# Softcap attention with a maxout layer: a ring of three pairs of PSUM banks and fewer, longer visits per pair of heads

## The chip, the cores and the metric

The kernel runs on one core of a Trainium2 chip. The metric is the device time in microseconds. Before the change the median of three runs is 359.17 us (359.16 to 360.23). The profiled execution took 359.29 us, of which the profile covers a span of 357.5 us; all times in the profile are counted from the start of this span.

## The reference, cut to what matters

```python
batch, n_heads, seq, head_dim = (8, 12, 448, 64)
n_tokens, d_model, d_ff = (3584, 768, 1024)

def _attn_ref(q, k, v, cap):
    scale = 1.0 / np.sqrt(q.shape[-1])
    scores = scale * np.matmul(q, k.transpose(0, 1, 3, 2))
    scores = cap * np.tanh(scores / cap)
    scores = scores - np.max(scores, axis=-1, keepdims=True)
    attn = np.exp(scores)
    attn = attn / (np.sum(attn, axis=-1, keepdims=True) + 1e-09)
    return np.matmul(attn, v).astype(np.float32)

def _moe_ref(x, w1, w2, w_out):
    h1 = x @ w1
    h2 = x @ w2
    g = np.maximum(h1, h2)
    return (g @ w_out).astype(np.float32)
# x: the attention's output, heads side by side, 3584 x 768
```

There are 96 heads. Each has 448 x 448 scores, which go through tanh and exp, are summed over the keys and multiplied with the values. Then every token goes through two matrices, an elementwise maximum and a third matrix. The kernel computes the maximum as relu(x @ (w1 - w2)) + x @ w2, and multiplies w2 with w_out once, so the second layer is x @ (w1 - w2), a relu, and x @ (w2 @ w_out) + relu @ w_out.

## The kernel before

The kernel works with the scores transposed: keys lie on partitions, queries along the row. The 448 keys of a head are three blocks of 128 and one of 64; the 64 left keys of two neighbouring heads share one block. One pass of the main loop, t, handles two pairs of heads (`ab` = 0, 1), four heads in all. TensorE computes scores into PSUM, ScalarE reads them through tanh into SBUF and then takes exp, and TensorE uses the exp for the sums over the keys and for the products with the values. VectorE adds the exp of the blocks, takes reciprocals and multiplies.

[...]Scores use two tiles of two banks each, the sums and the two halves of the values two banks, the second layer the last two:

```python
    s_psum = ctx.enter_context(tc.tile_pool(name="s_psum", bufs=2, space=PSUM))
    pv_psum = ctx.enter_context(tc.tile_pool(name="pv_psum", bufs=1, space=PSUM))
    mm_psum = ctx.enter_context(tc.tile_pool(name="mm_psum", bufs=2, space=PSUM))
```

The six full key blocks and the left block of a pass are spread over four parts, two score tiles in each of three parts and one tile in part 2. There is one exp for each part:

```python
    PARTS = (((0, 0), (0, 1)), ((0, 2), (1, 0)), ((0, 3), (1, 3)), ((1, 1), (1, 2)))
    ...
    def scores(t, p, m0=0, m1=2):
        if m0 == 0:
            tanh[t, p] = att.tile([P, 4, S], bf16, name="tanh")
        if p == 2:
            s = s_psum.tile([P, 2, 512], f32, name="s")
        for m, (ab, j) in list(enumerate(PARTS[p]))[m0:m1]:
            ...
            if p == 2:
                nc.tensor.matmul(s[:, m, :S], k0[:, 3 * P : 4 * P], qTn)          # L301
                continue
            s = s_psum.tile([P, 2, 512], f32, name="s")
            for h in range(2):
                r = slice(64 * h, 64 * h + 64)
                nc.tensor.matmul(s[:, h, :S], k0[r, j * P : (j + 1) * P], qTn[r, :])   # L306
            nc.scalar.activation(tanh[t, p][:, 2 * m : 2 * m + 2, :], s[:, :, :S], AF.Tanh, scale=scale / cap)  # L307
        if p == 2:
            nc.scalar.activation(tanh[t, p][:, 0:2, :], s[:, :, :S], AF.Tanh, scale=scale / cap)   # L309

    def ex(t, p):
        n = 2 if p == 2 else 4
        expo[t, p] = att.tile([P, n, S], bf16, name=f"expo{p}", bufs=2)
        nc.scalar.activation(expo[t, p], tanh[t, p][:, 0:n, :], AF.Exp, scale=float(cap))   # L314
```

The sums (`total`) and the two halves of the values (`values`) use matmuls of 32 columns, four side by side. Then the reciprocal and the product are VectorE's:

```python
    def total(t):
        ss = pv_psum.tile([P, 512], f32, name="ss")
        ...
            for ab, h, r in HEADS:
                nc.tensor.matmul(ss[r, :S], ones[:, :32], esum[t][:, 2 * ab + h, :], start=True, stop=True)   # L356
        ...   # VectorE: transpose, reciprocal, transpose, into inv[t]

    def values(t):
        out = []
        for u, bank in enumerate(("pv", "ss")):
            ps = pv_psum.tile([P, 512], f32, name=bank)
            ...   # 12 matmuls with vp (L372), 4 with vl (L378)
            out.append(ps)
        return out

    def normalize(t, ps):
        for u in range(2):
            nc.vector.tensor_mul(x_of(t, u), ps[u][:, :S], inv[t])
```

The second layer of earlier tokens is a queue of single matmuls (`moe`, lines L406, L418 and L421). `F(n)` takes n of them from the queue and puts them into TensorE's program at that place; what is left at the end follows in one piece. The order is the program's own: nothing is rescheduled. The main loop, cut to the order of these calls for t over 2:

```python
    for t in range(1, NQ):
        if more: scores(t + 1, 0)
        ex(t, 3);               F(6)
        ...                     # loads, transposing DMA
        F(8); add(t, 1, 0); F(2)
        if more: scores(t + 1, 1); ex(t + 1, 0)
        F(4); add(t, 1, 1); F(4); add(t, 0, 2); F(4); add(t, 1, 2); F(4)
        if more: scores(t + 1, 2); ex(t + 1, 1); F(5); add(t + 1, 0, 0)
        F(5)
        total(t)
        if more: scores(t + 1, 3); ex(t + 1, 2); add(t + 1, 0, 1)
        normalize(t, values(t))
        ...                     # casts on GpSimd
        F(3)
    F(10 ** 9)
```

Of the kernel before, what the change touches and what calls it, by code (L numbers as in the profile page):

```python
# [10 lines left out]
def kernel(  # L11
# [11 lines left out]
    nc = tc.nc  # L23
# [26 lines left out]
    xpool = ctx.enter_context(tc.tile_pool(name="xpool", bufs=2))  # L50
    opool = ctx.enter_context(tc.tile_pool(name="opool", bufs=OB))
    s_psum = ctx.enter_context(tc.tile_pool(name="s_psum", bufs=2, space=PSUM))
    pv_psum = ctx.enter_context(tc.tile_pool(name="pv_psum", bufs=1, space=PSUM))
    mm_psum = ctx.enter_context(tc.tile_pool(name="mm_psum", bufs=2, space=PSUM))


# [8 lines left out]
    vl = [const.tile([P, L, P], bf16, name=f"vl{i}") for i in range(2)]  # L65
    ones = const.tile([P, 64], bf16, name="ones")
    ones2 = const.tile([P, 2, 64], bf16, name="ones2")
    mark = const.tile([1, 1], bf16, name="mark")


    kqf = [const.tile([P, L, 8, P], bf16, name=f"kqf{i}") for i in range(2)]
# [210 lines left out]

    PARTS = (((0, 0), (0, 1)), ((0, 2), (1, 0)), ((0, 3), (1, 3)), ((1, 1), (1, 2)))
    LP = {c: (p, 2 * m if p != 2 else m) for p, cs in enumerate(PARTS) for m, c in enumerate(cs)}

    def scores(t, p, m0=0, m1=2):

        if m0 == 0:  # L290
            tanh[t, p] = att.tile([P, 4, S], bf16, name="tanh")
        if p == 2:
            s = s_psum.tile([P, 2, 512], f32, name="s")
        for m, (ab, j) in list(enumerate(PARTS[p]))[m0:m1]:
            i = 2 * t + ab
            g = i // L
            k0 = qkT[g][:, i % L, :, :].rearrange("p j c -> p (j c)")
            o = Q0 + (64 * (i // NP % 2) if g >= NT else 0)
            qTn = k0[:, o : o + S]
            if p == 2:  # L300
                nc.tensor.matmul(s[:, m, :S], k0[:, 3 * P : 4 * P], qTn)  # L301
                continue
            s = s_psum.tile([P, 2, 512], f32, name="s")
            for h in range(2):
                r = slice(64 * h, 64 * h + 64)
                nc.tensor.matmul(s[:, h, :S], k0[r, j * P : (j + 1) * P], qTn[r, :])  # L306
            nc.scalar.activation(tanh[t, p][:, 2 * m : 2 * m + 2, :], s[:, :, :S], AF.Tanh, scale=scale / cap)  # L307
        if p == 2:
            nc.scalar.activation(tanh[t, p][:, 0:2, :], s[:, :, :S], AF.Tanh, scale=scale / cap)  # L309

    def ex(t, p):
        n = 2 if p == 2 else 4
        expo[t, p] = att.tile([P, n, S], bf16, name=f"expo{p}", bufs=2)
        nc.scalar.activation(expo[t, p], tanh[t, p][:, 0:n, :], AF.Exp, scale=float(cap))  # L314

    def e_of(t, ab, j):
        p, m = LP[ab, j]
        return expo[t, p][:, m : m + (1 if j == NJ else 2), :]

    esum = {}  # L320

    def add(t, ab, step):

        if t < NS or t >= NQ:
            return
        if t not in esum:
            esum[t] = att.tile([P, 4, S], bf16, name="esum")
        d = esum[t][:, 2 * ab : 2 * ab + 2, :]
        if step == 2:

            r = slice(64 * ab, 64 * ab + 64)
            d = esum[t][r, ab::2, :]
            nc.vector.tensor_add(d, d, expo[t, 2][r, :, :])  # L333
        elif step == 0:
            nc.vector.tensor_add(d, e_of(t, ab, 1 if ab else 0), e_of(t, ab, 2 if ab else 1))  # L335
        else:
            nc.vector.tensor_add(d, d, e_of(t, ab, 0 if ab else 2))  # L337

    HEADS = [(m // 2, m % 2, slice(32 * m, 32 * m + 32)) for m in range(4)]
    NB = S // 32  # L340
# [1 line left out]

    def total(t):

        ss = pv_psum.tile([P, 512], f32, name="ss")
        if t < NS:
            for j in range(NJ):
                for ab, h, r in HEADS:
                    nc.tensor.matmul(
                        ss[r, :S], ones[:, :32], e_of(t, ab, j)[:, h, :], start=(j == 0), stop=False  # L350
                    )
            for ab, h, r in HEADS:
                nc.tensor.matmul(ss[r, :S], ones2[:, h, :32], expo[t, 2][:, ab, :], start=False, stop=True)
        else:
            for ab, h, r in HEADS:
                nc.tensor.matmul(ss[r, :S], ones[:, :32], esum[t][:, 2 * ab + h, :], start=True, stop=True)  # L356
        st = att.tile([P, NB, 32], f32, name="st", bufs=1)
        nc.vector.transpose(st.rearrange("p b c -> p (b c)"), ss[:, :S])  # L358
        rs = att.tile([P, NB, 1], f32, name="rs", bufs=2)
        nc.vector.reciprocal(rs, st[:, :, 0:1])  # L360
        inv[t] = att.tile([P, S], f32, name="inv", bufs=2)
        nc.vector.transpose(inv[t].rearrange("p (b c) -> p b c", c=32), rs.to_broadcast([P, NB, 32]))

    def values(t):

        out = []
        for u, bank in enumerate(("pv", "ss")):
            ps = pv_psum.tile([P, 512], f32, name=bank)
            for j in range(NJ):
                for ab, h, r in HEADS:  # L370
                    g, n = divmod(2 * t + ab, L)
                    nc.tensor.matmul(  # L372
                        ps[r, :S], vp[g % 2][:, 2 * n + h, j, u::2], e_of(t, ab, j)[:, h, :],
                        start=(j == 0), stop=False,
                    )
            for ab, h, r in HEADS:
                g, n = divmod(2 * t + ab, L)
                nc.tensor.matmul(  # L378
                    ps[r, :S], vl[g % 2][:, n, 64 * h + u : 64 * h + 64 : 2], expo[t, 2][:, ab, :], start=False, stop=True
                )  # L380
            out.append(ps)
        return out

    xT = {}
# [6 lines left out]

    def normalize(t, ps):
        for u in range(2):
            nc.vector.tensor_mul(x_of(t, u), ps[u][:, :S], inv[t])  # L394

    gT = {}

# [98 lines left out]
    cast(nc.vector, 0, "k", 1, L)  # L496
    cast(nc.vector, 0, "q", 1, L)
    scores(0, 0)
    scores(0, 1, 0, 1)
    ex(0, 0)  # L500
    transposes(1)
    scores(0, 1, 1, 2)
    ex(0, 1)
    transposes(2)
    scores(0, 2)
    ex(0, 2)
    for _ in turn_w2(0):
        pass
    scores(0, 3)
    ex(0, 3)  # L510
    cast(nc.gpsimd, 1, "k")
    cast(nc.gpsimd, 1, "q")
    for c in range(2, KC):
# [9 lines left out]

    def premultiply_first(f0, f1):
        if f0 == 0:
            first[0] = pv_psum.tile([P, 512], f32, name="pv")
            first[1] = pv_psum.tile([P, 512], f32, name="ss")
        for f in range(f0, f1):
            for half in range(2):
                nc.tensor.matmul(  # L530
                    first[half][:, : DM // 2],
                    w2T[0][:, f * P : (f + 1) * P],
                    wo_sb[:, f, half * (DM // 2) : (half + 1) * (DM // 2)],
                    start=(f == 0), stop=(f == FC - 1),
                )
        if f1 == FC:
            for half in range(2):
                nc.vector.tensor_copy(
                    wm_sb[:, 0, half * (DM // 2) : (half + 1) * (DM // 2)], first[half][:, : DM // 2]
                )  # L540
# [10 lines left out]
    cast(nc.gpsimd, 1, "v")  # L551
    cast(nc.gpsimd, 2, "k")
    cast(nc.gpsimd, 2, "q")
    premultiply_first(0, 2)
    scores(1, 1)
    ex(1, 0)
    premultiply_first(2, 4)
    transposes(4)
    scores(1, 2)
    ex(1, 1)  # L560
    premultiply_first(4, 6)
    transposes(5)
    scores(1, 3)
    ex(1, 2)
    cross(2)
    load(3, "k")
    load(3, "q")
# [2 lines left out]
    for c in range(1, KC):  # L570
        if c + 1 < KC:
            fill_q.append(turn_w2(c + 1))
        fill_q.append(premultiply(c))
    scores(2, 0)
    ex(1, 3)
    total(0)
    F(3)
    normalize(0, values(0))
    F(2)

    for t in range(1, NQ):
        i = 2 * t
        more = t + 1 < NQ
        F(24 if t == 2 else 0)
        if t > 1 and more:
            scores(t + 1, 0)
        if t > 1:
            ex(t, 3)
            F(6)
        if t in crosses:  # L590
            cross(crosses[t])
# [7 lines left out]
            cast(nc.gpsimd, 3, "v")  # L599
        if t > 2:  # L600
            extra(i)
        F(8 if t > 1 else 0)
        add(t, 1, 0)
        F(2 if t > 1 else 0)
        if more:
            scores(t + 1, 1)
            ex(t + 1, 0)
        F(4)
        add(t, 1, 1)
        F(4)  # L610
        if t == 2:
            cast(nc.gpsimd, 2, "v")
            load(3, "v")
        add(t, 0, 2)
        F(4)
        add(t, 1, 2)
        F(4)
        if more:
            scores(t + 1, 2)
            ex(t + 1, 1)  # L620
            F(5)
            add(t + 1, 0, 0)
        if t == 1:
            for c in range(4):
                subtract(c, nc.gpsimd)
# [2 lines left out]
            extra(5)  # L628
        if t > 2:
            extra(i + 1)  # L630
        F(5)
        total(t)
        if more:
            scores(t + 1, 3)
            ex(t + 1, 2)
            add(t + 1, 0, 1)
        else:
            F(12)
        normalize(t, values(t))
        if casts[t]:  # L640
            nc.gpsimd.tensor_copy(mark, x_of(t, 1)[:1, :1])  # L641
            for g, what in casts[t]:
                cast(nc.gpsimd, g, what)
        if t % 3 == 2:
            fill_q.append(moe(t // 3))
        F(3)
    F(10 ** 9)
# [1 line left out]
_INS = ['q', 'k', 'v', 'cap', 'moe_w1', 'moe_w2', 'moe_w_out']  # L649
# [31 lines left out]
```

## Time and profile before

| what | before |
|---|---|
| device time, median | 359.17 us |
| span of the profile | 357.5 us |
| tanh, 128 x 896, from PSUM (L307 and L309) | 144 of 914 ns and 24 of 916 ns |
| exp, 128 x 1792 / 128 x 896 (L314) | 72 of 1695 ns / 24 of 952 ns |
| score matmuls (L306 / L301) | 288 / 48 |
| matmuls of the second layer (L406, L418, L421) | 384, 336, 448 |
| TensorE waited for a tanh before a score matmul (L306) | 1.8 us, 5 times |
| ScalarE waited for scores (L307 / L309) | 16.0 us, 15 times / 5.5 us, 7 times |

A busy share says how long an engine had an instruction running. Matmuls overlap each other, so TensorE's busy time is read with care, and the distance from one start to the next says what one of them really costs. A wait is put down to the instruction that ended last before the waiting one began. "PE" is TensorE's matmuls, "ACT" is ScalarE, "DVE" is VectorE, and L306 means line 306 of the kernel. A row of the timeline has the start in us, the length, the engine, the line, the operation, output and input, how many of them are merged, and in brackets the idle time before it with what ended it.

Most of ScalarE's 16.0 us of waits for scores is one wait of 6.8 us that ends at 48.56 us, where the first transposed keys come by DMA.

### The profile page before, as it was taken

What the parts mean: (1) busy time and instruction counts of PE and PEld (TensorE: products, weight loads), DVE (VectorE), ACT (ScalarE), POOL (GpSimd) and SP (SyncE); (2) the same over time, 40 slices, a digit from 0 to 9 for tenths busy, and PEclk for the clock granted to TensorE, in tenths of its full rate; (3) what the DMA queues carried; (4) which work ended last, traced back from release to release, by engine and by line L of the source; (5) the groups of instructions that cost most, each with busy time, mean ns of one, the idle gap of its engine ahead of it and who ended that gap; (6) DMA issues with size and microseconds to landing.
All of it is one profiled execution on the core that took longest, in us unless ns stands there. A gap on an engine that the chain in (4) does not pass through costs nothing.

```text
span 357.5 us, 6788 instructions
## 1 busy us (share of the span) xinstructions
PE 336.5 (94%) x2710; PEld 163.5 (46%) x2710; DVE 227.3 (64%) x410; ACT 281.5 (79%) x265; POOL 108.3 (30%) x172
## 2 busy tenths in 40 slices
PE   3899869899999999999999999999999999999996
PEld 2444424444444444445444554444445444455563
DVE  4336607777767776786688565976786667843421
ACT  3989639899999999999999999999999999200000
POOL 6554848231244124303430443034304400000000
PEclk9999969999999999999999999999999999999999
DMA  7999997948796869675977498948982511012022
GB/s 252 245 251 246 345 253 168 271 92 209 109 300 156 196 126 303 193 167 96 294 217 166 81 266 261 197 94 233 272 190 57 155 72 65 0 46 89 0 90 88
DMA packets 103200, 61.79 MB, mean 173 GB/s; under 512 B 62336, under 2 KB 98176, under 8 KB 103168
## 3 DMA queue, kind: packets, MB, share of 16 engines
q1 hardware_dynamic: 101216, 58.21, 62.6%
q0 software_dynamic: 1952, 3.15, 4.9%
q8 instruction: 21, 0.34, 0.4%
q14 instruction: 11, 0.09, 0.1%
HBM read 42.47 MB, written 11.01 MB: 150 GB/s over the span
## 4 chain that ended last, share of the span: by engine, by line
PE 42%; ACT 36%; DMA 13%; DVE 7%; issue 1%; SPq 0%; DVEq 0%; ACTq 0%
ACT expo L314 17%; ACT tanh L307 16%; PE mm L406 13%; PE mm L421 10%; DMA kr<-in_k_dram 9%; PE mm L418 8%; PE s L306 4%; ACT tanh L309 3%; DMA qkT<-kqf 3%; DVE gT L410 2%; PE pv L372 2%; PE ss L372 2%; DMA osb<-in_moe_w_dram 1%; DVE esum L333 1%; PE mm L243 1%
## 5 line engine op out<-in xcount | busy, mean ns | idle before, releaser
L314 ACT ACTIVATE expo<-tanh 128x1792 bf16<-128x1792 bf16 (+1 forms) x96 | 144.8, 1509 | 0.1
L307 ACT ACTIVATE tanh<-s 128x896 bf16<-128x896 f32 x144 | 124.2, 914 | 17.9 <-PE s L306 16.0
L421 PE MATMUL mm<-wo_sb,gT 128*128 128x384 bf16 x448 | 86.8, 327 | 0.0
L406 PE MATMUL mm<-xT,wd_sb 128*128 128x448 bf16 x384 | 80.2, 353 | 4.1 <-DVE gT L410 3.0
L418 PE MATMUL mm<-wm_sb,xT 128*128 128x384 bf16 x336 | 66.7, 327 | 0.2 <-DVE gT L410 0.2
L421 PEld LDWEIGHTS <-gT 128*128 128x128 bf16 x448 | 42.0, 98 | 34.2 <-issue 8.0
L406 PEld LDWEIGHTS <-wd_sb 128*128 128x128 bf16 x384 | 35.9, 98 | 44.1 <-issue 13.8
L425 DVE COPY osb<-mm 128x384 f32<-128x384 f32 x56 | 31.0, 554 | 37.0 <-PE mm L421 36.6
L306 PE MATMUL s<-qkT 64*128 64x448 bf16 x288 | 43.6, 371 | 7.7 <-DMA qkT<-kqf 4.2
L335 DVE TENSOR_TENSOR esum<-expo 128x896 bf16<-128x896 bf16 x42 | 29.4, 699 | 32.7 <-ACT expo L314 32.2
L410 DVE TENSOR_SCALAR gT<-mm 128x448 bf16<-128x448 f32 x64 | 39.6, 621 | 14.2 <-PE mm L406 13.8
L641 POOL COPY mark<-xT 1x1 bf16<-1x1 bf16 x18 | 3.2, 179 | 147.5 <-DVE xT L394 122.0
L418 PEld LDWEIGHTS <-xT 128*128 128x128 bf16 x336 | 31.8, 98 | 26.7 <-issue 6.6
L309 ACT ACTIVATE tanh<-s 128x896 bf16<-128x896 f32 x24 | 22.0, 916 | 6.0 <-PE s L301 5.5
L333 DVE TENSOR_TENSOR esum<-esum,expo 64x896 bf16<-64x896 bf16 x42 | 25.9, 617 | 0.9
L337 DVE TENSOR_TENSOR esum<-esum,expo 128x896 bf16<-128x896 bf16 x42 | 25.6, 610 | 0.3
L306 PEld LDWEIGHTS <-qkT 64*128 64x128 bf16 x288 | 9.7, 95 | 31.6 <-issue 24.2
L358 DVE STREAM_TRANSPOSE st<-ss 128x448 f32<-128x448 f32 x24 | 15.6, 649 | 8.8 <-PE ss L356 6.4
L372 PEld LDWEIGHTS <-vp 128*32 128x32 bf16 x576 | 13.3, 96 | 16.2 <-issue 8.3
L183 POOL CAST kqf<-kr 128x1152 bf16<-128x1152 f32 x14 | 15.9, 1138 | 9.0 <-DMA kr<-in_k_dram 5.0
L372 PE MATMUL pv<-expo,vp 128*32 128x448 bf16 x288 | 18.1, 356 | 0.0
L372 PE MATMUL ss<-expo,vp 128*32 128x448 bf16 x288 | 17.8, 352 | 0.0
(70 smaller groups left out, 275.5 us busy)
## 6 DMA issues: line engine op xcount, KB each, us to landing
kr<-in_k_dram SPq DMA_DIRECT2D x14, 576.0 KB, 6.6
qr<-in_q_dram SPq DMA_DIRECT2D x14, 576.0 KB, 7.1
vr<-in_v_dram SPq DMA_DIRECT2D x14, 576.0 KB, 4.9
out_dram<-osb SPq DMA_DIRECT2D x20, 384.0 KB, 4.7
out_dram<-osb SPq DMA_DIRECT2D x16, 192.0 KB, 4.2
osb<-in_moe_w_dram SPq DMA_DIRECT2D x4, 512.0 KB, 8.5
gT<-in_moe_w_dram POOLq DMA_DIRECT2D x6, 256.0 KB, 12.3
wo_sb<-in_moe_w_out_dram POOLq DMA_DIRECT2D x4, 384.0 KB, 16.2
```

The source lines that it names most:

```text
L306: nc.tensor.matmul(s[:, h, :S], k0[r, j * P : (j + 1) * P], qTn[r, :])
L307: nc.scalar.activation(tanh[t, p][:, 2 * m : 2 * m + 2, :], s[:, :, :S], AF.Tanh, scale=scale / cap)
L309: nc.scalar.activation(tanh[t, p][:, 0:2, :], s[:, :, :S], AF.Tanh, scale=scale / cap)
L314: nc.scalar.activation(expo[t, p], tanh[t, p][:, 0:n, :], AF.Exp, scale=float(cap))
L333: nc.vector.tensor_add(d, d, expo[t, 2][r, :, :])
L335: nc.vector.tensor_add(d, e_of(t, ab, 1 if ab else 0), e_of(t, ab, 2 if ab else 1))
L372: nc.tensor.matmul(ps[r, :S], vp[g % 2][:, 2 * n + h, j, u::2], e_of(t, ab, j)[:, h, :], start=(j == 0), stop=False,)
L406: nc.tensor.matmul(ps[:, :S], wd_sb[:, c, f * P : (f + 1) * P], x[:, c, cs], start=(c == 0), stop=(c == KC - 1))
L410: nc.vector.tensor_relu(g[:, f, cs], ps[:, :S])
L418: nc.tensor.matmul(ps[:, : DM // 2], x[:, c, ts], wm_sb[:, c, hs], start=(c == 0), stop=False)
L421: nc.tensor.matmul(ps[:, : DM // 2], g[:, f, ts], wo_sb[:, f, hs], start=False, stop=(f == FC - 1))
L425: nc.vector.tensor_copy(osb[:, hs], ps[:, : DM // 2])
```

## The change

The change makes four parts into three. Parts 0 and 1 hold the three full key blocks of one pair of heads each, and part 2 holds the left block of both. Parts 0 and 1 have three score tiles and one exp over six key parts of 448; part 2 stays as it was. There are thus three exps in a pass instead of four.

The PSUM banks become a ring of three pairs. The third score tile of parts 0 and 1 is put into the pair of banks that the values also use (`v_psum`), and the sums take a tile of `s_psum`. Sums, values and left scores follow each other on TensorE with no other matmul between them, so that TensorE changes the shape of its matmuls less often. The calls of F are shared out anew; there are 45 in a pass for t over 2, as before, and 12 instead of 5 at t = 0.

```diff
-    pv_psum = ctx.enter_context(tc.tile_pool(name="pv_psum", bufs=1, space=PSUM))
+    v_psum = ctx.enter_context(tc.tile_pool(name="v_psum", bufs=1, space=PSUM))
...
-    PARTS = (((0, 0), (0, 1)), ((0, 2), (1, 0)), ((0, 3), (1, 3)), ((1, 1), (1, 2)))
...
+    def two_banks(pool):
+        return pool.tile([P, 2, 512], f32, name="s" if pool is s_psum else "v")
+
+    def scores(t, p, last=None):
+
+        tanh[t, p] = att.tile([P, 2 * NJ, S], bf16, name="tanh")
+        for j in range(NJ if p < 2 else 1):
+            s = two_banks(last if last and j == NJ - 1 else s_psum)
+            for m in range(2):
+                i = 2 * t + (p if p < 2 else m)
...
+                if p == 2:
+                    nc.tensor.matmul(s[:, m, :S], k0[:, 3 * P : 4 * P], qTn)
+                else:
+                    r = slice(64 * m, 64 * m + 64)
+                    nc.tensor.matmul(s[:, m, :S], k0[r, j * P : (j + 1) * P], qTn[r, :])
+            nc.scalar.activation(tanh[t, p][:, 2 * j : 2 * j + 2, :], s[:, :, :S], AF.Tanh, scale=scale / cap)
 
     def ex(t, p):
-        n = 2 if p == 2 else 4
+        n = 2 * NJ if p < 2 else 2
...
     def total(t):
 
-        ss = pv_psum.tile([P, 512], f32, name="ss")
+        ss = two_banks(s_psum)[:, 0, :]
...
     def values(t):
 
-        out = []
-        for u, bank in enumerate(("pv", "ss")):
-            ps = pv_psum.tile([P, 512], f32, name=bank)
+        out = two_banks(v_psum)
+        for u in range(2):
+            ps = out[:, u, :]
...
-    F(3)
+    F(4)
     normalize(0, values(0))
-    F(2)
+    F(8)
 
     for t in range(1, NQ):
...
-        F(24 if t == 2 else 0)
-        if t > 1 and more:
-            scores(t + 1, 0)
         if t > 1:
-            ex(t, 3)
+            F(24 if t == 2 else 0)
+            if more:
+                scores(t + 1, 0, v_psum)
+            ex(t, 2)
             F(6)
...
-        F(8 if t > 1 else 0)
-        add(t, 1, 0)
-        F(2 if t > 1 else 0)
+        if t > 1:
+            F(2)
+            add(t, 0, 0)
+            F(3)
+            add(t, 0, 1)
+            F(3)
+            add(t, 1, 0)
+            F(2)
         if more:
-            scores(t + 1, 1)
-            ex(t + 1, 0)
-        F(4)
+            scores(t + 1, 1, v_psum)
+            ex(t + 1, 0) if t > 1 else None
+        F(3)
         add(t, 1, 1)
         F(4)
...
+        F(3)
         add(t, 0, 2)
         F(4)
         add(t, 1, 2)
-        F(4)
-        if more:
-            scores(t + 1, 2)
-            ex(t + 1, 1)
-            F(5)
-            add(t + 1, 0, 0)
...
-        F(5)
+        F(10)
         total(t)
+        ps = values(t)
         if more:
-            scores(t + 1, 3)
-            ex(t + 1, 2)
-            add(t + 1, 0, 1)
-        else:
-            F(12)
-        normalize(t, values(t))
+            scores(t + 1, 2)
+            ex(t + 1, 1)
+        normalize(t, ps)
         if casts[t]:
-            nc.gpsimd.tensor_copy(mark, x_of(t, 1)[:1, :1])
+            nc.gpsimd.tensor_copy(mark, inv[t][:1, :1])
...
-        F(3)
+        F(5)
     F(10 ** 9)
```

The start of the program is reordered in the same way: the scores of the first two passes are issued by whole pairs of heads.

More of the change, by code (lines that the diff above doesn't have):

```diff
@@ L67 @@
     ones2 = const.tile([P, 2, 64], bf16, name="ones2")
-    mark = const.tile([1, 1], bf16, name="mark")
+    mark = const.tile([1, 1], f32, name="mark")
     kqf = [const.tile([P, L, 8, P], bf16, name=f"kqf{i}") for i in range(2)]
@@ L281, in cross @@
         )
-    PARTS = (((0, 0), (0, 1)), ((0, 2), (1, 0)), ((0, 3), (1, 3)), ((1, 1), (1, 2)))
[L286 to L309, printed above, removed]
@@ new lines, in two_banks @@
+    def two_banks(pool):
[6 more added lines that the diff above has]
+                i = 2 * t + (p if p < 2 else m)
+                g = i // L
+                k0 = qkT[g][:, i % L, :, :].rearrange("p j c -> p (j c)")
+                o = Q0 + (64 * (i // NP % 2) if g >= NT else 0)
+                qTn = k0[:, o : o + S]
+                if p == 2:
[4 more added lines that the diff above has]
+            nc.scalar.activation(tanh[t, p][:, 2 * j : 2 * j + 2, :], s[:, :, :S], AF.Tanh, scale=scale / cap)
@@ L316, in e_of @@
     def e_of(t, ab, j):
-        p, m = LP[ab, j]
-        return expo[t, p][:, m : m + (1 if j == NJ else 2), :]
+        return expo[t, ab][:, 2 * j : 2 * j + 2, :]
     esum = {}
@@ L334, in add @@
         elif step == 0:
-            nc.vector.tensor_add(d, e_of(t, ab, 1 if ab else 0), e_of(t, ab, 2 if ab else 1))
+            nc.vector.tensor_add(d, e_of(t, ab, 0), e_of(t, ab, 1))
         else:
-            nc.vector.tensor_add(d, d, e_of(t, ab, 0 if ab else 2))
+            nc.vector.tensor_add(d, d, e_of(t, ab, 2))
     HEADS = [(m // 2, m % 2, slice(32 * m, 32 * m + 32)) for m in range(4)]
@@ L380, in values @@
                 )
-            out.append(ps)
         return out
@@ L393, in normalize @@
         for u in range(2):
-            nc.vector.tensor_mul(x_of(t, u), ps[u][:, :S], inv[t])
+            nc.vector.tensor_mul(x_of(t, u), ps[:, u, :S], inv[t])
     gT = {}
@@ L498 @@
     scores(0, 0)
-    scores(0, 1, 0, 1)
     ex(0, 0)
     transposes(1)
-    scores(0, 1, 1, 2)
+    scores(0, 1)
     ex(0, 1)
     transposes(2)
+    for _ in turn_w2(0):
+        pass
     scores(0, 2)
     ex(0, 2)
[L507 to L510, printed above, removed]
     cast(nc.gpsimd, 1, "k")
@@ L525, in premultiply_first @@
         if f0 == 0:
-            first[0] = pv_psum.tile([P, 512], f32, name="pv")
-            first[1] = pv_psum.tile([P, 512], f32, name="ss")
+            both = two_banks(v_psum)
+            for half in range(2):
+                first[half] = both[:, half, :]
         for f in range(f0, f1):
@@ L553 @@
     cast(nc.gpsimd, 2, "q")
+    ex(1, 0)
     premultiply_first(0, 2)
     scores(1, 1)
-    ex(1, 0)
+    ex(1, 1)
     premultiply_first(2, 4)
     transposes(4)
+    premultiply_first(4, 6)
     scores(1, 2)
-    ex(1, 1)
-    premultiply_first(4, 6)
+    ex(1, 2)
     transposes(5)
-    scores(1, 3)
-    ex(1, 2)
     cross(2)
@@ L573 @@
         fill_q.append(premultiply(c))
+    total(0)
     scores(2, 0)
-    ex(1, 3)
-    total(0)
-    F(3)
+    ex(2, 0)
+    F(4)
     normalize(0, values(0))
-    F(2)
+    F(8)
     for t in range(1, NQ):
```

## The prediction

> **What bounds the kernel now.** I call one pass of the main loop (t to t+1: two pairs of heads, that is four heads) a period, each group of score matmuls that TensorE does in one go a visit, and the dense matmuls that F(n) puts between visits fills. The page comes first, its busy shares and then its slices.
>
> ```profile
> PE 336.5 (94%) x2710; PEld 163.5 (46%) x2710; DVE 227.3 (64%) x410; ACT 281.5 (79%) x265; POOL 108.3 (30%) x172
> PE   3899869899999999999999999999999999999996
> ACT  3989639899999999999999999999999999200000
> PEclk9999969999999999999999999999999999999999
> ```
>
> From slice 7 to slice 33 both TensorE and ScalarE read nine tenths; then ScalarE is done and TensorE alone runs off the remaining fills. One stage has two engines near their limit, the tail has one. The chain that ended last agrees: PE 42%, ACT 36%. So the second view is ScalarE's timeline over one period:
>
> ```profile
> 192.40 1.69 ACT L314 ACTIVATE expo<-tanh 128x1792 bf16<-128x1792 bf16 x1
> 194.12 1.73 ACT L307 ACTIVATE tanh<-s 128x896 bf16<-128x896 f32 x2
> 195.73 0.95 ACT L314 ACTIVATE expo<-tanh 128x896 bf16<-128x896 bf16 x1
> 196.71 1.73 ACT L307 ACTIVATE tanh<-s 128x896 bf16<-128x896 f32 x2
> ...
> 204.20 1.69 ACT L314 ACTIVATE expo<-tanh 128x1792 bf16<-128x1792 bf16 x1
> ```
>
> There is no gap. A tanh takes 0.805 from start to start (194.12 to 195.73 for two), the wide exp 1.72 up to the next tanh, the narrow one 0.98. Seven tanh, three wide exps and one narrow make 5.64 + 5.16 + 0.98 = 11.78; measured 192.40 to 204.20 = 11.80. ScalarE sets most periods. Over a longer stretch the mean is longer: the first tanh of (t=4, visit 0) starts at 62.26, that of t=23 at 292.90, so 230.64 / 19 = 12.14. The excess is found as a wait on some visits:
>
> ```profile
> 191.58 0.92 ACT L309 ACTIVATE tanh<-s 128x896 bf16<-128x896 f32 x1 [0.69 <-PE s L301]
> 227.78 0.92 ACT L309 ACTIVATE tanh<-s 128x896 bf16<-128x896 f32 x1 [0.81 <-PE s L301]
> ```
>
> ScalarE waits for a visit that TensorE reaches late. The third view is TensorE's own timeline around a visit:
>
> ```profile
> 195.46 0.66 PE L421 MATMUL mm<-wo_sb,gT 128*128 128x384 bf16 x3
> 196.05 0.55 PE L306 MATMUL s<-qkT 64*128 64x448 bf16 x4
> 196.54 1.15 PE L418 MATMUL mm<-wm_sb,xT 128*128 128x384 bf16 x6
> 197.52 1.46 PE L421 MATMUL mm<-wo_sb,gT 128*128 128x384 bf16 x8
> 198.82 0.49 PE L418 MATMUL mm<-wm_sb,xT 128*128 128x384 bf16 x2
> ...
> 219.51 0.37 PE L306 MATMUL s<-qkT 64*128 64x448 bf16 x2 [0.23 <-ACT tanh L307]
> 219.81 1.47 PE L421 MATMUL mm<-wo_sb,gT 128*128 128x384 bf16 x8
> ```
>
> The printed lengths overlap, so I read starts. Eight 384-column fills take 197.52 to 198.82, 0.1625 each; the 48 of 448 columns from 326.68 to 335.76 take 0.189. Three fills from 195.46 stream until 195.95, the scores start at 196.05: 0.10 to change shape. Four score matmuls run as two pairs of 0.19, to 196.42, and the next fill starts at 196.54: 0.12 to change back. The last two lines show TensorE waiting for a score bank: the tanh that held it ended at 219.46, the pair started 0.05 later, the fills 0.30 after that.
>
> **What the Trainium skill says.** "TensorEngine Tiling (Array Packing)", Key Properties: changing the tiling mode drains TensorE. The trace agrees; here it costs the 0.10 to 0.12 above. "ScalarE: Activation LUTs", What ACT_TABLE_LOAD costs: an ACTIVATE with immediate scale and bias takes 186 ns plus 0.833 ns per element, and neighbours overlap by about 93 ns. The trace: exp of 896 and 1792 elements take 952 and 1695 ns, so 0.83 per element and 209 fixed; tanh overlaps the next by 914 - 805 = 109. "TensorE: Matmul & The Clock Gate", Why this matters for your kernels, warns of gaps in TensorE's work over about 3 us. The trace has one of 4.21 us, ended at 47.90 by a transposing DMA, and the mean clock from 40 to 60 us is 0.83; after the 1.33 us gap that ends at 67.77 the clock from 60 to 100 is 1.00.
>
> **The change part by part.**
>
> ScalarE loses one exp per period. An exp over 2688 elements extrapolates to 1.695 + 0.743 = 2.44, 2.46 with the gap to the next tanh. Two of these, seven tanh and one narrow exp make 4.92 + 5.64 + 0.98 = 11.54, so 0.24 less per period. Alone that would be worth some 5 us.
>
> TensorE loses two shape changes per period. Before, visits 0 and 1 cost two each, visit 2 none (full shape, like fills), and sums, visit 3 and values four: eight. After: two, two, and two for sums, values and left scores in one go: six. Some 0.22 less per period, beside ScalarE.
>
> The ring gets three pairs of banks, call them A, B (s_psum) and V (v_psum). Per period TensorE fills visit 0: A, B, V; visit 1: A, B, V; sums: A; values: V; left scores: B. V has one buffer, so visit 1's last pair waits for visit 0's third tanh; the built instruction order shows that wait on ScalarE. So visit 1 cannot be finished ahead of ScalarE by more than one tile. Between visits 1 and 2 the order has 24 fills, between 0 and 1 16, and between 2 and the next 0 five. The sum, 45, is the same as before (10, 3, 16, 16).
>
> I follow one period from the end of visit 0's third tanh. TensorE: 0.05 hand-over, 0.30 for V's pair and the shape change, 24 fills at 0.171 (mean by counts: 784 of 384 columns, 384 of 448) = 4.10, shape change 0.10, sums 0.19, values 1.54 (two banks; 193.83 to 195.37 in the trace), shape change 0.10, then 0.63 from the first left score to its tanh (190.95 to 191.58). Together 7.01. In this time ScalarE has the narrow exp 0.98, three tanh 2.42 and the six-part exp 2.46: 5.86, less 0.11 overlap = 5.75. It runs dry and waits about 1.25. Then ScalarE: left tanh 0.805, exp 2.46, tanh 0.805, 0.805 and the full 0.914 = 5.79, and the loop closes: 12.80 per period. TensorE meanwhile arrives early at visit 1 (5 fills, visit 0 and 16 fills end some 11.2 after the start) and waits until 12.0 for B and 12.8 for V. Both engines wait about 1.3 per period, in turn. VectorE's evacuations add a little: TensorE waited 3.0 + 0.9 us for them in all, 0.16 per period, of which 24/45 fall in this stretch: 0.09. Period 12.9 against 12.14.
>
> The same arithmetic on the kernel before, as a test: from the end of visit 0's last tanh TensorE needs 0.35 + 16 fills + 0.63 to the left scores, 3.6 with 384-column fills and 4.0 with the others; ScalarE has 0.98 + 1.61 + 1.72 - 0.11 = 4.2 to do. So no wait, except where 448-column fills also wait for VectorE (0.74 at 224.88): 4.74 - 4.2 = 0.5, where the trace has 0.81 at 227.78. The method fits within some 0.3.
>
> Sum: up to the gap at 43.7 to 47.9 everything waits for the DMA, so the reordered start is free. After it TensorE runs at half pace for about 5 us (14 fills take 4.5). Through that first period I get 51.1 for the third tanh, 54.9 for V's pair, 61.4 for the left tanh, 64.7 for the first tanh of t=4 (62.26 now). Nineteen periods of 12.9 give 309.8 for that of t=23. The sums of t=22 follow 2.53 + 0.35 + 4.10 + 0.10 = 7.1 later. From there the kernel before needed 357.5 - 301.02 = 56.5 with 280 fills; now 275 are left (seven more are put into the start, and of each period two more come after the sums), 0.8 less. End 309.8 + 7.1 + 55.7 = 372.6; the time is 1.7 above the span: 374.3.
>
> **The rivals.** (a) The gain comes through: ScalarE sets the pace at 11.54 plus the old excess, some 0.24 x 20 = 5 us less, 354. For it: ScalarE is gapless now and TensorE has 0.22 less to do. Against: the loop above; it needs at most 24 - 1.25/0.171, about 17, fills between visits 1 and 2, and there are 24. (b) About equal, 357 to 362: TensorE arrives at visit 1 late anyway, or the waits eat just the gain. It would need TensorE's sum to be the bound; but TensorE's own work per period, 45 x 0.171 = 7.7 of fills, 1.52 of scores, 0.19 of sums, 1.54 of values and six shape changes of 0.11, is 11.6, well under the loop's 12.8, so it does arrive early. (c) Much slower, 390 and more: the new gaps pull the clock down. Against: the 1.33 us gap above did not. (d) V comes free late for visit 0, since normalize holds it: two transposes, a reciprocal and two multiplies end about 3.2 after the sums start, visit 0 wants V 3.6 after, and ScalarE is still in an exp for 2 more. Small.
>
> **Range and chances.** With nothing but 384-column fills the period is 12.6, with only 448-column ones 13.24; 19 periods put these at 368.6 and 380.8. The start's half-pace stretch may move it by 2. I take 367.5 to 380.5. Within 2% ends at 366.4, so slower by over 2% has 0.87, within 0.09, faster 0.04.
>
> **What would show it.** Right: ScalarE waits of 1 to 1.5 us for the left scores in nearly every period (20 of them, 20 to 28 us in all), TensorE waits on tanh at visit 1 of the same size, ScalarE busy about 276, the exp of 2688 elements at 2.44, periods near 12.9, clock near 1.00. Wrong: ScalarE gapless after a wide exp, or TensorE never waiting at visit 1, or a period under 12; or a new wait of visit 0 on VectorE's multiply.

## The result, and the profile after

| | before | after |
|---|---|---|
| device time, median | 359.17 us | 372.18 us |
| range of the runs | 358.69 to 360.23 | 371.89 to 373.8 |
| ratio | 1 | 1.0367 (95%: 1.033 to 1.0405) |
| span of the profile | 357.5 us | 370.3 us |
| ScalarE busy | 281.5 us | 277.2 us |
| exps | 72 of 1695 ns, 24 of 952 ns | 48 of 2445 ns, 24 of 960 ns |
| ScalarE waited for left scores | 5.5 us, 7 times | 33.4 us, 23 times |
| TensorE waited for a tanh at a visit | 1.8 us, 5 times | 20.9 us, 40 times |
| mean period, left tanh to left tanh, t = 3 to 23 | 12.12 us | 12.90 us |

The change is slower by 3.7%. It did what it says: ScalarE has 24 instructions and 4.3 us less to do. Both engines now stand idle in places where they did not before. The first view is the page of the changed kernel, busy shares and slices.

```profile
PE 336.5 (91%) x2710; PEld 167.3 (45%) x2710; DVE 227.2 (61%) x410; ACT 277.2 (75%) x241; POOL 111.3 (30%) x172
PE   3679989999999998999999999999999999999996
ACT  3997677798889889788988988798898889500000
```

ScalarE's row has eights and sevens where it had nines. TensorE's row still shows nines: a slice is 9.3 us and a digit of nine covers 90% and more, so waits of about 0.9 us in 12.9 hardly show. The table of waits shows them (columns: us in total, times, longest):

```profile
ACT tanh L304 <- PE s L300: 33.4, 23, 3.4
PE s L303 <- ACT tanh L304: 12.0, 20, 1.6
PE v L303 <- ACT tanh L304: 8.9, 20, 0.4
```

ScalarE waits for the left scores (L300) in every pass from t = 3 on, and TensorE waits for tanh at the third tile of visit 1 in nearly every pass and at the second in most: from 60 to 300 us 8.5 us in 19 waits and 5.9 us in 14; the rest of its 20.9 us stands in the start. So each of the two engines waits for the other in nearly every period. The timelines show how. First ScalarE, one period:

```profile
214.38 0.92 ACT L304 ACTIVATE tanh<-s 128x896 bf16<-128x896 f32 x1 [1.09 <-PE s L300]
215.19 2.44 ACT L309 ACTIVATE expo<-tanh 128x2688 bf16<-128x2688 bf16 x1
217.66 1.73 ACT L304 ACTIVATE tanh<-s 128x896 bf16<-128x896 f32 x2
219.27 0.92 ACT L304 ACTIVATE tanh<-v 128x896 bf16<-128x896 f32 x1
...
223.47 2.46 ACT L309 ACTIVATE expo<-tanh 128x2688 bf16<-128x2688 bf16 x1
227.02 0.92 ACT L304 ACTIVATE tanh<-s 128x896 bf16<-128x896 f32 x1 [1.09 <-PE s L300]
```

Then TensorE in the same stretch:

```profile
218.63 0.36 PE L303 MATMUL s<-qkT 64*128 64x448 bf16 x2
219.44 0.36 PE L303 MATMUL s<-qkT 64*128 64x448 bf16 x2 [0.44 <-ACT tanh L304]
220.25 0.36 PE L303 MATMUL v<-qkT 64*128 64x448 bf16 x2 [0.45 <-ACT tanh L304]
220.54 0.50 PE L414 MATMUL mm<-wo_sb,gT 128*128 128x384 bf16 x2
...
224.55 0.37 PE L350 MATMUL s<-esum,ones 128*32 128x448 bf16 x4
...
226.37 0.55 PE L300 MATMUL s<-qkT 128*128 128x448 bf16 x2
```

TensorE is at visit 1 early. Its three pairs start 0.81 apart, exactly ScalarE's spacing of the tanh of visit 0: each pair is let in by one tanh. The pair in `v` starts at 220.25, the third tanh having ended at 219.27 + 0.92 = 220.19. Only then can the 24 fills begin, at 220.54. They, the sums and the values take until 226.37, the left scores' tanh starts at 227.02, and ScalarE, whose six-part exp ended at 223.47 + 2.46 = 225.93, has been idle for 1.09.

### The profile page after: what moved, and what is told of

The parts are those of the page before. It is cut to its first block, busy times and chain, and to the rows that moved or that the text cites. A ratio compares the mean times of both kernels' runs of the same rounds, so it can differ in the third digit from the quotient of the medians.

```text
span 370.3 us, 6777 instructions
## 1 busy us (share of the span) xinstructions
PE 336.5 (91%) x2710; PEld 167.3 (45%) x2710; DVE 227.2 (61%) x410; ACT 277.2 (75%) x241; POOL 111.3 (30%) x172
## 4 chain that ended last, share of the span: by engine, by line
PE 52%; ACT 29%; DMA 12%; DVE 3%; issue 2%; SPq 0%; ACTq 0%; DVEq 0%
ACT tanh L304 17%; PE mm L414 14%; ACT expo L309 11%; PE mm L399 11%; PE mm L411 10%; DMA kr<-in_k_dram 8%; PE v L366 6%; DMA qkT<-kqf 3%; PE s L300 3%; PE v L303 2%; PE v L372 2%; PE s L350 2%; PE mm L243 2%; DMA osb<-in_moe_w_dram 1%; DVE gT L403 1%
## 5 line engine op out<-in xcount | busy, mean ns | idle before, releaser
L304 ACT ACTIVATE tanh<-s 128x896 bf16<-128x896 f32 x125 | 108.8, 914 | 43.0 <-PE s L300 33.4
L309 ACT ACTIVATE expo<-tanh 128x2688 bf16<-128x2688 bf16 (+1 forms) x72 | 140.3, 1950 | 0.8 <-PE v L366 0.6
L303 PE MATMUL s<-qkT 64*128 64x448 bf16 x202 | 35.7, 373 | 15.9 <-ACT tanh L304 12.0
L629 POOL COPY mark<-inv 1x1 f32<-1x1 f32 x18 | 3.2, 178 | 154.3 <-DVE inv L356 137.0
L303 PEld LDWEIGHTS <-qkT 64*128 64x128 bf16 x288 | 13.7, 94 | 58.6 <-issue 52.6
L304 ACT ACTIVATE tanh<-v 128x896 bf16<-128x896 f32 x43 | 39.7, 923 | 0.0
L366 PE MATMUL v<-expo,vp 128*32 128x448 bf16 x576 | 35.6, 353 | 0.0
L387 DVE TENSOR_TENSOR xT<-v,inv 128x448 bf16<-128x448 f32 x48 | 27.7, 619 | 4.7 <-PE v L372 2.0
L352 DVE STREAM_TRANSPOSE st<-s 128x448 f32<-128x448 f32 x24 | 15.6, 649 | 17.7 <-PE s L350 15.9
L303 PE MATMUL v<-qkT 64*128 64x448 bf16 x86 | 15.6, 351 | 8.9 <-ACT tanh L304 8.9
```

The lines of the kernel that those rows point to most:

```text
L303: nc.tensor.matmul(s[:, m, :S], k0[r, j * P : (j + 1) * P], qTn[r, :])
L304: nc.scalar.activation(tanh[t, p][:, 2 * j : 2 * j + 2, :], s[:, :, :S], AF.Tanh, scale=scale / cap)
L366: nc.tensor.matmul(ps[r, :S], vp[g % 2][:, 2 * n + h, j, u::2], e_of(t, ab, j)[:, h, :], start=(j == 0), stop=False,)
L387: nc.vector.tensor_mul(x_of(t, u), ps[:, u, :S], inv[t])
```

## Experiments

All kernels are the changed kernel with one edit, or, where the name says so, with the left scores first and one edit more. "Fills" is the number of dense matmuls between visit 1 and what follows it (24 in the changed kernel); the pass keeps 45 unless said otherwise. The periods are those from left tanh to left tanh; "384" is the value that repeats in passes with 384-column fills, "mean" is over t = 3 to 23.

| kernel | median us | ratio to before (95%) | period, 384 / mean |
|---|---|---|---|
| before | 358.8 to 359.2 | 1 | 11.81 / 12.12 |
| changed | 372.18 | 1.0367 (1.033 to 1.0405) | 12.64 / 12.90 |
| changed, again | 371.74 | 1.0376 (1.0345 to 1.0406) | 12.64 / 12.90 |
| 17 fills | 351.67 | 0.9819 (0.978 to 0.9858) | 11.57 / 11.91 |
| 20 fills | 359.36 | 1.0019 (1.0001 to 1.0036) | 11.99 / 12.28 |
| 28 fills | 385.07 | 1.0732 (1.0695 to 1.0769) | 13.29 / 13.57 |
| 30 fills, 47 in a pass | 384.42 | 1.0713 (1.0686 to 1.0739) | 13.61 / 13.85 |
| left scores first | 352.55 | 0.9845 (0.979 to 0.9901) | 11.58 / 11.89 |
| left scores first, again | 352.16 | 0.9807 (0.9781 to 0.9833) | 11.58 / 11.90 |
| left scores between sums and values | 352.6 | 0.983 (0.9804 to 0.9855) | 11.58 / 11.89 |
| exp of part 0 split | 373.31 | 1.0421 (1.0392 to 1.045) | 12.64 / 12.92 |
| exp of part 1 split | 374.33 | 1.0436 (1.0411 to 1.0462) | 12.73 / 12.99 |
| left first, both exps split | 352.96 | 0.9837 (0.9806 to 0.9867) | 11.76 / 11.90 |
| left first, fills weighted | 353.47 | 0.9865 (0.9837 to 0.9894) | 11.80 / 11.91 |

The theory is that of the prediction: visit 1 is tied to the tanh of visit 0 by the third pair of banks, and the work that TensorE has between visit 1 and the left scores is longer than what ScalarE has in hand. The rivals are VectorE's multiplies, which hold the third pair, and TensorE's sum of work, for which the place of the fills would not matter.

### The dose: 20, 17, 28 fills

```diff
 # scores(t + 1, 1, v_psum); ex(t + 1, 0)      24 -> 20           24 -> 17
-        F(3); add(t, 1, 1); F(4)            # F(2), F(3)         F(1), F(3)
-        F(3); add(t, 0, 2); F(4)            # F(3), F(3)         F(2), F(3)
-        add(t, 1, 2); F(10)                 # F(9)               F(8)
 # total, values, left scores, normalize
-        F(5)                                # F(9)               F(12)
```

> Theory (ring and pace: visit 1's last pair waits for visit 0's third tanh, and the 24 fills that follow make the left scores late): four fills fewer in that stretch shorten the period by 4 x 0.171 = 0.68, 12.9 to 12.2, over 20 periods 13.7 us: 358.5. ScalarE's waits for left scores fall from about 1.1 to 0.4. Rival (VectorE: the pair V comes free late through the multiplies, so visit 0 sets the period): the place of the fills does not matter, 372 within 2. Rival (sum of work: TensorE's drains, fills and gaps add up wherever the fills stand): 372 within 2.

Measured: 359.36, equal to the kernel before. Passes with 384-column fills went from 12.64 to 11.99, by 0.65 = 4 x 0.1625. ScalarE's waits for left scores went from 33.4 to 18.7 us in all, in such passes from 1.09 to 0.45.

> Theory: at 17 fills TensorE brings the left scores as ScalarE ends the six-part exp, so the wait is gone and ScalarE's own 11.54 with some 0.2 of other waits sets the period: 11.75, 20 x 1.15 less than after, 349 (346 to 353). ScalarE without gaps except where 448-column fills stand. Both rivals: 372 within 2.

Measured: 351.67, inside the range, but 2.7 above its middle: passes with 384-column fills take 11.57, where ScalarE has no wait (its own sum of work is 11.54 by the prediction's arithmetic), while the mean is 11.91 and not 11.75.

> Theory: four fills more lengthen the period by 0.68: 386 (384 to 388), and each wait for the left scores grows to 1.8. Both rivals: 372 within 2.

The kernel that ran under this name was not the one meant: it had F(5), F(5), F(5), F(5), F(10), so 30 fills in the stretch and 47 in a pass. Six more fills should give 12.64 + 6 x 0.1625 = 13.61, and 13.61 is what the trace has. The time, 384.42, contains another effect: two more fills in each of some 20 passes are 40 fewer in the tail. That it lies in the expected range is therefore an accident. The next kernel has the 28 that were meant.

```diff
-        F(3); add(t, 1, 1); F(4); ... F(3); add(t, 0, 2); F(4); add(t, 1, 2); F(10)
+        F(4); add(t, 1, 1); F(5); ... F(4); add(t, 0, 2); F(5); add(t, 1, 2); F(10)
-        F(5)
+        F(1)
```

> Really four fills more between visit 1 and the sums (28, and one instead of five after the left scores, 45 in a pass); the run called e3_fills28 had 30 there and 47 in a pass. Theory: period 12.64 + 4 x 0.1625 = 13.29 in passes with 384-column fills, 20 x 0.68 = 13.7 us more than the changed kernel: 385.5. Rivals: 372.

Measured: 385.07 and 13.29. Over 17, 20, 24, 28 and 30 fills the period in the 384-column passes is 11.57, 11.99, 12.64, 13.29, 13.61: a straight line of 0.162 per fill, which is the spacing of one fill, down to a floor: at 17 the line would give 11.50, and ScalarE without a gap needs 11.57. Neither rival gives a slope. The ring alone does not make the kernel slower either: with 17 fills it has the same three pairs and the same order of tiles, TensorE waits for a tanh at V's pair only 1.0 us in 6 passes, and the kernel takes 351.67 against 358.95 before. No kernel here lets visit 1 run further ahead with 24 fills in place; that the tie to the third tanh is needed for the loss is read from the timeline.

### Left scores ahead of the sums

```diff
+        if more:
+            scores(t + 1, 2)
         total(t)
         ps = values(t)
         if more:
-            scores(t + 1, 2)
             ex(t + 1, 1)
```

> Left scores go ahead of the sums and values, with no other shape change; 24 fills stay. Theory: the left tanh can start 0.10 + 0.19 + 1.54 + 0.10 = 1.9 earlier, more than the wait of 1.1 to 1.3, so the wait is gone and ScalarE sets the period at about 11.75: 349 (346 to 353). Rival (VectorE frees V late): the sums start 0.38 later, so the period grows by as much: 372 to 380. Rival (sum of work): 372 within 2.

Measured: 352.55, and 352.16 when repeated: inside the range, 3.5 above the 349 at its middle, since the mean period is 11.89 and not 11.75. The 24 fills and the ring are as in the changed kernel; the left scores have the fills' shape, so there are still six shape changes. ScalarE's timeline of this kernel:

```profile
198.03 2.46 ACT L309 ACTIVATE expo<-tanh 128x2688 bf16<-128x2688 bf16 x1
200.52 0.92 ACT L304 ACTIVATE tanh<-s 128x896 bf16<-128x896 f32 x1
201.34 2.44 ACT L309 ACTIVATE expo<-tanh 128x2688 bf16<-128x2688 bf16 x1
...
212.10 0.92 ACT L304 ACTIVATE tanh<-s 128x896 bf16<-128x896 f32 x1
```

The left tanh starts 0.03 after the six-part exp ended at 200.49; the wait is gone, and the period is 200.52 to 212.10 = 11.58. Moving two matmuls ahead of 36 others (4 of the sums, 32 of the values) changed the time by 5%. VectorE did not lengthen the period as its rival said, though it shows: visit 0's pair in `v` is held up by a multiply, in one pass by 0.48.

```profile
215.46 0.36 PE L303 MATMUL v<-qkT 64*128 64x448 bf16 x2 [0.48 <-DVE xT L387]
```

### Which exp lies on the loop

```diff
-        nc.scalar.activation(expo[t, p], tanh[t, p][:, 0:n, :], AF.Exp, scale=float(cap))
+        for a, b in ((0, 4), (4, n)) if p == 0 else ((0, n),):      # or p == 1
+            nc.scalar.activation(expo[t, p][:, a:b, :], tanh[t, p][:, a:b, :], AF.Exp, scale=float(cap))
```

> The changed kernel once more, as the reference for the two splits beside it: 372 within 1.5.

Measured: 371.74.

> The six-part exp of part 0 alone is done as two exps of four and two parts; it costs ScalarE 0.209 fixed less some 0.12 overlap, 0.09 per pass. Theory: this exp lies in the stretch in which ScalarE waits for the left scores, so the wait shrinks by 0.09 and the time stays, within 0.5 of the changed kernel. Rival (ScalarE's sum of work sets the time, as before the change): 22 x 0.09 = 2 us more.

In the trace the period stays at 12.64 and the wait shrinks from 1.09 to 1.00, as expected:

```profile
211.16 2.55 ACT L310 ACTIVATE expo<-tanh 128x1792 bf16<-128x1792 bf16 x2
214.72 0.92 ACT L304 ACTIVATE tanh<-s 128x896 bf16<-128x896 f32 x1 [1.00 <-PE s L300]
```

The median does not fit so well: 373.31, 1.6 above the changed kernel and outside the 0.5 that was expected. The two intervals (1.0392 to 1.045 and 1.0345 to 1.0406) overlap, and the profiled executions have spans of 370.6 and 370.5. So the time by itself doesn't settle it; the period does.

> The six-part exp of part 1 alone is split in the same way. Theory: this exp lies on the loop (left tanh, exp of part 1, tanh of visit 0, V's pair, fills, left scores), so the period grows by 0.09: 20 x 0.09 = 1.8 us more than the changed kernel. Rival (both engines have room, the fills alone set the time): within 0.5 of the changed kernel.

Measured: 374.33, 2.6 more, with an interval above that of the changed kernel. The period went to 12.73, by 0.09, and the wait stayed 1.09. The two exps are alike and cost ScalarE the same; only the one on the loop lengthens the period.

### What bounds the mended kernel

```diff
 # left first:  split both six-part exps (p < 2), as above
 # left first:  F counts by duration
-                next(fill_q[0])
-                rate[1] -= 1
+                rate[1] -= next(fill_q[0]) or 1     # moe yields 1.105 (448 columns) or 0.95 (384)
 # changed kernel: left scores between
         total(t)
+        if more:
+            scores(t + 1, 2)
         ps = values(t)
```

> The kernel with the left scores ahead of sums and values once more, as the reference for the two beside it: 352.5 within 1.

Measured: 352.16.

> Left scores first, and both six-part exps split into four and two parts: ScalarE has 2 x 0.09 = 0.18 more per pass, TensorE nothing. If ScalarE's work sets the period there: 22 x 0.18 = 4 us more than with the left scores first, 356.5. If TensorE's sum of work does: unchanged, 352.5. If passes with 384-column fills (two of three) belong to ScalarE and the others to TensorE: 2.7 more, 355.

Measured: 352.96, and the mean period is 11.90 as without the split. The passes with 384-column fills did become 0.18 longer, 11.58 to 11.76, so ScalarE sets those. The others became shorter (the longest 13.05 to 12.36), and nothing is left in the mean. The third case, in which the two kinds of pass add up independently, does not hold: what ScalarE adds in one kind of pass comes off the waits of the other.

> As the kernel with the left scores first, but F counts a 448-column fill as 1.105 and a 384-column fill as 0.95 (their spacings of 0.189 and 0.1625 over the mean of 0.171), so each stretch between visits is equally long on TensorE. Theory: the waits that are left with the left scores first stand in the passes with 448-column fills (19 us of waits for scores in all, of which some 6 from 60 us on); evening them out takes about half of these: 349 to 351 against 352.5. Rival (what is left is VectorE's evacuation of the 448-column fills): 352 to 353, unchanged.

Measured: 353.47. The passes are evener, 11.65 to 12.21 instead of 11.57 to 13.05, and the mean is 11.91. Evening out gains nothing. The rival's number (unchanged) came closer; its cause, VectorE's evacuation, is not shown by this run.

> The changed kernel with the left scores between the sums and the values: two more changes of shape (0.22 per pass, as many as before the change), the left tanh 1.54 earlier than in the changed kernel. Theory: 1.54 is more than ScalarE's wait of 1.1, so the wait goes: 352.5 if ScalarE then sets the period, 352.5 + 20 x 0.22 = 357 if TensorE's sum of work does, 354 if it does so in one pass of three. Rival (VectorE or the fills set the changed kernel's time): 372 or more.

Measured: 352.6; the wait is gone and the mean is 11.89. From 60 to 300 us TensorE of this kernel was busy 239.3 of 240 us, with no wait for a tanh; with the left scores first it was 237.1, with the changed kernel 224.6. The next lines are the windows of this kernel (columns: window, its length, busy us and instructions of TensorE's matmuls, its weight loads, VectorE, ScalarE and GpSimd, then clock, DMA share, GB/s):

```profile
100.00:150.00 50.00, 49.80 (x395) 23.16 (x395) 38.63 (x69) 48.05 (x43) 15.70 (x25) 1.00 0.79 206
150.00:200.00 50.00, 50.00 (x398) 23.79 (x396) 36.88 (x66) 48.16 (x43) 14.73 (x25) 1.00 0.73 175
```

The mean of 11.9 appears in five mended kernels. That two more shape changes did not lengthen it is against my 357, and taken by itself against TensorE's sum as the bound. The traces of the two kernels say why. From the last fill ahead of sums, values and left scores to the first fill behind them TensorE needs 2.46 with the left scores first and 2.68 with them between (means of 20 passes from 60 to 300 us): the two shape changes cost their 0.22. But from the first pair of visit 0 to the next fill it needs 0.94 with the left scores first and only 0.72 with them between, since the sums come 0.38 earlier and so do VectorE's multiplies: weight loads of visit 0 wait for these 10.6 us in this stretch in the one kernel, 5.6 in the other. The two differences cancel. So both runs fit TensorE's own work, with what it waits for VectorE, as what paces the mended kernels in the mean; this is worked out from the traces, and no run lengthens TensorE's work alone. It stays open which part of the change makes the mended kernels 7 us faster than the kernel before: splitting the exps again cost 0.8 and two more shape changes 0.4, neither outside the spread of the runs. A part that shows in the traces belongs to neither: from 60 to 300 us TensorE waited 3.5 us for VectorE to empty banks of the second layer before the change, 0.8 with the left scores first and 0.6 with them between.

## Why the prediction was right

It said 374.3 (367.5 to 380.5), with 0.87 for slower by over 2%. Measured: 372.18. By its steps:

**Bounds before.** That ScalarE sets the pace in most passes is a little too much: from t = 3 on, 9 of the 20 periods before the change are its own 11.80 or 11.81, the others 11.91 to 13.35. That TensorE is close behind holds. (One slice of the stretch that is said to read nine reads eight for both engines; nothing rests on it.)

**The parts.** The six-part exp was put at 2.44 and measured 2.445; ScalarE busy 276 against 277.2. ScalarE's saving was real and went into waits. TensorE's two shape changes are not seen in the time of any run: putting two back left the period where it was, for the reason given above.

**The loop.** The period was 12.60 for 384-column fills and 12.9 in the mean; measured 12.64 and 12.90. The straight line over the number of fills shows that the stretch between V's pair and the left scores is the cause, and the gain from moving the left scores shows it from the other side. The "about 17" fills that the prediction named as the most that fit is where the line meets the floor.

**The waits.** ScalarE's wait for left scores was put at 1 to 1.5 in nearly every period, 20 to 28 us. Measured: 27.1 us over the 20 passes from t = 4 on (33.4 with those of the start), 1.09 in the 384-column passes, but 1.30 to 2.15 where fills of 448 columns stand. TensorE's waits at visit 1, put at the same size, were smaller: 0.89 in a 384-column pass, 14.3 us from 60 to 300 us. Its own work is thus some 11.75 in such a pass (12.64 less 0.89), where the prediction's mean had 11.6.

**The start.** This is the mis-sized term. (ScalarE's wait of 6.8 us there is the longest of its 16.0 us of waits for scores before the change, not most of them.) The prediction let TensorE run at half pace for about 5 us after the gap that ends near 48 us, and put the first tanh of t = 4 at 64.7; it came at 62.85. From there all agrees: 307.82 - 62.85 = 244.97 for nineteen periods, 12.89 each, against 12.9; and 62.5 from there to the end against 62.8. The miss of 2.1 us in the time is in the main the 1.9 of this term. What happened instead is in TensorE's timeline, before the change and after it:

```profile
47.90 0.93 PE L306 MATMUL s<-qkT 64*128 64x448 bf16 x4 [4.21 <-DMA qkT<-kqf]
48.76 4.52 PE L243 MATMUL mm<-wo_sb,w2T 128*128 128x384 bf16 x14
```

```profile
48.97 0.55 PE L303 MATMUL s<-qkT 64*128 64x448 bf16 x4 [1.12 <-DMA qkT<-kqf]
...
52.53 4.07 PE L243 MATMUL mm<-wo_sb,w2T 128*128 128x384 bf16 x24
```

The gap was 1.12 instead of 4.21, since TensorE's work ahead of it ended later (47.85 against 43.68), and after it 24 fills took 4.0 us, full pace; before the change 14 took 4.4 there. V's pair, which the prediction put at 54.9, came at 52.25. The granted clock from 40 to 60 us was 1.00 (0.83 before). So the step that failed is that a half-pace stretch follows the gap. Of the thirteen traces with the new start, with gaps of 0.71 to 2.55 at this place, two have one: with 17 fills (gap 2.21) and with weighted fills (2.41) the matmuls from 50.5 us on are some 0.3 apart for about 2 us. The execution of the kernel with 17 fills that has it took 354.12, its other three 351.31 to 351.82.

From 20 to 40 us the granted clock was 0.74 in the changed kernel and 1.00 before, but this is not the slow stretch moved ahead: before the change the 384-column matmuls from 18.33 to 25.69 stand some 0.3 apart within their groups too, as those from 20.40 to 28.08 do after it. "The reordered start is free" was nearly right: the transposing DMA was issued at 38.70 as before (38.67), and the wait for it ended at 48.97 instead of 47.90; why it took longer is open.

**The rivals.** (a), a gain of 5 us, fell because of the wait it did not count; the kernel with 17 fills shows that it comes, and somewhat larger, once this wait is out. (b) would have needed TensorE to arrive late at visit 1; it arrived early. (c), a lower clock through the new gaps: TensorE waits 0.4 to 0.5 twice per pass, and the clock stays at 1.00 from 60 us on. "TensorE: Matmul & The Clock Gate" in the Trainium skill (Why this matters for your kernels) warns of gaps of over about 3 us. Waits far below that left the clock alone here, but not everywhere: in the start of the changed kernel it fell from 1.00 between 15 and 20 us to 0.51 between 20 and 25 us, and no wait of TensorE from 4 us to there was longer than 1.6 us. The matmuls agree: 26 small ones take 0.60 at 19.72 and 0.84 at 26.20. (d), VectorE holding V, does not show in the waits of the changed kernel from 60 us on, and shows with the left scores first, as above.

## What to carry to other kernels

When a ring of buffers is as long as one visit, the producer can't run ahead of the consumer, so what the producer does between two visits must be shorter than what the consumer has in hand; count both sides of that stretch, not the sum over the loop. Put the matmuls that another engine waits for at the front of a group, and those that nobody waits for behind them. Saving fixed costs on an engine that had no gap is worth nothing if the same edit takes away the work that it could do while it waits.

## What was not expected of the hardware

Two more shape changes per pass, 0.10 to 0.12 each, left the period at 11.89 where it was 11.90: TensorE needed 0.22 more for them and waited as much less for VectorE.

The granted clock of the profile does not show every stretch at half pace. With the left scores first it reads 1.00 from 20 to 28 us, and the 384-column matmuls there start some 0.3 apart within their groups, against 0.1625 in the main loop; before the change the same holds from 18.33 to 25.69. The changed kernel has that pace there with a granted clock of 0.51 from 20 to 25 us. The granted clock of this stretch is not the same in every execution of one kernel either: with the left scores first it was 1.00 from 20 to 30 us in one trace and 0.83 in the other. The distance from one start to the next is the safer measure of the pace.
